# Changing the layout of y, the engine that stores results, and the order of the opening in a gated linear attention kernel with an MLP behind it

## The chip, the cores and the metric

One core of one Trainium2 chip. The metric is the device time of one execution in microseconds (us), as the median of three runs.

## The reference, cut to what matters

A recurrent attention over 768 tokens (4 batches, 8 heads, head size 48) with a decay per channel, and an MLP with a SiLU between two matrices (384 to 2048 to 384) on its 3072 output rows.

```python
B, H, S, D = 4, 8, 768, 48
f = 1.0 / (1.0 + np.exp(-f_logit))
for t in range(S):
    state = f[:, :, t, :, None] * state + np.einsum('bhd,bhe->bhde', k[:, :, t], v[:, :, t])
    y[:, :, t] = np.einsum('bhd,bhde->bhe', q[:, :, t], state)
x = y.transpose(0, 2, 1, 3).reshape(B * S, H * D)
h = x @ w_in
g = h * (1.0 / (1.0 + np.exp(-h)))
out = g @ w_out
```

## The kernel before, in words

The tokens are cut into 6 chunks (g) of 128 per batch; with 4 batches (b) there are 24 units (g, b). Heads are taken in pairs (p, 4 of them), two heads of 64 padded channels on the 128 partitions. For each unit:

- `decay` (L138): the log decays are summed over tokens by one matmul with a triangle (`cs`, one PSUM buffer); ACT makes exp(cs) and exp(-cs) from it (L144, L147); POOL scales k into `ki` (L145), DVE scales q into `qg` (L148). `values` (L150) casts v to bf16 on POOL, or on ACT where told.
- `transposes` (L171): 8 transposes into one PSUM buffer, evacuated by DVE (L178).
- `scores` (L181): 8 matmuls into one PSUM buffer; DVE masks them in two operations (`atm`, L190).
- `outputs` (L193): y is made with channels on partitions, ready to be the moving operand of the MLP, in 3 blocks of 128 channels. A head of 48 channels can straddle two blocks, so the v tile `vp` keeps zeros around every head and a window of 128 columns of it is the weight (10 matmuls), and the state tile `st` is 384 columns wide and zero outside the pair's block (6 matmuls, from chunk 1 on). DVE evacuates to `xT` (L209).
- `state` (L211): the old state goes into PSUM by a matmul with the identity (L217, from chunk 1 on), 4 matmuls add k times v (L220), and DVE multiplies by the chunk's last decay into `st` (L224, two operations).

The MLP: `mlp_in` (L252) does 3 matmuls for each of 16 blocks of hidden channels into one of two PSUM buffers (`h_ps`), ACT evacuates with SiLU (L266). `mlp_out` (L269) does 16 matmuls for each 128 rows into the same two buffers (`o_ps`), DVE copies to `o_sb` (three buffers, L278), and SP issues the store (L280). The loads of q, k, v and f are issued by SP too (L85), in program order with the stores, two buffers for each tensor; the weights are loaded by POOL (L109, L114).

The order on every engine is the order of the program. `run` interleaves streams: it always takes the next step of the stream that has used the smallest share of its stated cost. The costs (`T_COST` and so on, the numbers that the streams yield) have no other use. From chunk 1 on, while one chunk's `mlp_in` runs, half of the next chunk's attention (`attend`) is interleaved, and while its `mlp_out` runs, the other half together with `prep` (values, decay, lasts) of the chunk after that. `logs` (L129), which makes the log decays on ACT, needs the exp and ln tables, and stands ahead of that second half; SiLU needs other tables. Ahead of that loop an opening handles chunk 0 in two halves of two batches (FIRST, SECOND), then chunk 0's MLP and chunk 1.

Of the kernel before, what the change touches and what calls it, by code (L numbers as in the profile page):

```python
# [41 lines left out]
def kernel(  # L42
# [10 lines left out]
    nc = tc.nc  # L53
# [9 lines left out]
    VW = D + 128  # L63
# [34 lines left out]
    vp = [singles.tile([C, B, 128 + H * VW], BF16, name=f"vp{i}") for i in range(2)]  # L98
    st = [singles.tile([C, NP, HD], BF16, name=f"st{i}") for i in range(B)]
# [50 lines left out]
    def values(g, b, engine=None):  # L150
        src, dst = loaded[g, "v"][:, b], v_data(g % 2, b)
# [41 lines left out]
    def outputs(g, b):  # L193
        i = g % 2
        y_ps = yps.tile([128, KT, C], F32, name="y_ps", tag="yd")
        for t in range(KT):
            terms = []
            if g > 0:
                for p in range(NP):
                    if 2 * D * p < 128 * (t + 1) and 2 * D * (p + 1) > 128 * t:  # L200
                        terms.append((st[b][:, p, 128 * t:128 * (t + 1)], qkT[b][:, 0, p, :]))
            for h in range(H):
                if D * h < 128 * (t + 1) and D * (h + 1) > 128 * t:
                    terms.append((v_window(i, b, h, t), atm[b][:, h % 2, h // 2, :]))
            for n, (l, r) in enumerate(terms):
                nc.tensor.matmul(y_ps[:, t, :], l, r, start=(n == 0), stop=(n == len(terms) - 1))  # L206
        if g not in xT:
            xT[g] = gk.tile([128, KT, B, C], BF16, name="xT")
        nc.vector.tensor_copy(xT[g][:, :, b, :], y_ps)  # L209

    def state(g, b):  # L211
        i = g % 2
        flat = st[b].rearrange("p n w -> p (n w)")
        blocks = bass.AP(flat.tensor, flat.offset, [list(flat.ap[0]), [HD + 2 * D, NP], [1, 2 * D]])
        d_ps = yps.tile([128, NP, 2 * D], F32, name="d_ps", tag="yd")
        if g > 0:
            nc.tensor.matmul(d_ps, ident, blocks, start=True, stop=False, skip_group_check=True)  # L217
        vv = v_data(i, b)
        for p in range(NP):
            nc.tensor.matmul(d_ps[:, p, :], ki[i][:, b, 2 * p:2 * p + 2, :], vv[:, 2 * p:2 * p + 2],  # L220
                             start=(g == 0 and p == 0), stop=(p == NP - 1), skip_group_check=True)
        for r in range(2):
            lo = 64 * r
            nc.vector.tensor_mul(blocks[lo:lo + D, :, r * D:(r + 1) * D],  # L224
                                 d_ps[lo:lo + D, :, r * D:(r + 1) * D],
                                 alast[g][lo:lo + D, b, :, None].to_broadcast([D, NP, D]))

    T_COST, A_COST, Y_COST, D_COST = 450.0, 350.0, 900.0, 330.0

    def attend(g, lo, hi):  # L230

        units = range(lo, hi)
        for s in range(len(units) + 2):
# [35 lines left out]
    def mlp_out(g, lo, hi):  # L269
        for b in range(lo, hi):  # L270
            o_ps = hps.tile([C, d_model], F32, name="o_ps", tag="h_ps")
            for n in range(NT):
                nc.tensor.matmul(o_ps, hT[g][:, n, b * C:(b + 1) * C], w_out_sb[:, n, :],  # L273
                                 start=(n == 0), stop=(n == NT - 1))
                if n % 4 == 3 and n < NT - 1:
                    yield 650.0
            o_sb = op.tile([C, d_model], F32, name="o_sb")
            nc.vector.tensor_copy(o_sb, o_ps)  # L278
            r0 = b * S + g * C
            nc.sync.dma_start(out=out[r0:r0 + C, :], in_=o_sb)  # L280
            yield 650.0
# [4 lines left out]
    def prep(g, lo, hi):  # L286

        for b in range(lo, hi):
            values(g, b)
            decay(g, b)  # L290
            yield 200.0
        lasts(g, lo, hi)
        yield 120.0 * (hi - lo)

    def prep_cost(lo, hi):
        return (hi - lo) * 320.0
# [19 lines left out]
    def run(*streams):  # L316
        for _ in interleave_gen(*streams):
            pass

    with tc.manual_schedule():  # L320
# [15 lines left out]
        for b in range(*FIRST):  # L336
            values(0, b)
        logs(0, *SECOND)
        for b in range(*FIRST):
            transposes(0, b)  # L340
        for b in range(*SECOND):
            decay(0, b)
        for b in range(*FIRST):
            scores(0, b)
        load_w_in()
        for b in range(*FIRST):
            outputs(0, b)
# [11 lines left out]
        for b in range(*SECOND):  # L359
            outputs(0, b)  # L360
# [78 lines left out]
```

## Time and profile before

| what | us |
|---|---|
| median of 3 runs (lowest, highest) | 245.88 (244.97, 246.54) |
| the profiled execution | 248.17 |
| its span, from the first to the last instruction | 246.4 |

The rows below come from the profiled execution, whose time lies 1.8 us above its span. Engines: PE is the matrix engine (PEld its weight loads), DVE the vector engine, ACT the scalar engine, POOL GpSimd, SP the engine that only issues transfers (SPq, its queue). "PEclk" is the clock that was granted to PE, as a share of the full 2.4 GHz; 0.5 is the lower level, 1.2 GHz. A group row reads: line, engine, operation, output<-input, shapes, count | busy us, mean ns of one | idle time ahead of it <- what ended that.

### The profile page before, as it was taken

The numbers are of one execution on the slowest core, as the hardware profiler recorded it, in microseconds if no ns is written. First come the engines' busy times: TensorE is split into PE (matmuls) and PEld (weight loads), VectorE is DVE, ScalarE is ACT, GpSimd is POOL, SyncE is SP. The second block draws the span as 40 slices with busy tenths as digits, with TensorE's granted clock in tenths as the row PEclk, the third lists the DMA queues.
The fourth block names the chain that finished last, engine by engine and source line by source line (L and its number), as shares of the span: only waits on it lengthen the run. The fifth ranks groups of instructions, "written<-read, shape, count | busy, mean of one in ns | idle before, by whom it ended". The sixth has DMA issues, their size and how long they took to land.

```text
span 246.4 us, 4049 instructions
## 1 busy us (share of the span) xinstructions
PE 201.1 (82%) x1680; PEld 123.4 (50%) x1680; DVE 111.0 (45%) x193; ACT 114.3 (46%) x181; POOL 53.3 (22%) x65
## 2 busy tenths in 40 slices
PE   0346689968604896899779999999999999999994
PEld 0125534536304672687535565655666555663462
DVE  7727722246204544467655345763557453520011
ACT  4351237850410386348265683556735654008600
POOL 8629100050300006300190000900009100000000
PEclk9999769999965798589958999999999999999999
DMA  8999999999992000699409991179601100100011
GB/s 138 187 186 194 191 185 190 197 180 185 189 192 95 0 3 32 131 188 176 85 28 195 187 137 49 49 141 188 90 35 64 36 0 0 63 37 32 3 64 64
DMA packets 105971, 27.00 MB, mean 110 GB/s; under 512 B 99296, under 2 KB 105952, under 8 KB 105952
## 3 DMA queue, kind: packets, MB, share of 16 engines
q1 hardware_dynamic: 102272, 23.60, 60.3%
q0 software_dynamic: 3680, 3.15, 7.9%
q8 instruction: 13, 0.21, 0.4%
q14 instruction: 6, 0.05, 0.1%
HBM read 25.17 MB, written 4.72 MB: 121 GB/s over the span
## 4 chain that ended last, share of the span: by engine, by line
PE 77%; DMA 6%; DVE 5%; ACT 4%; SPq 4%; issue 2%; ACTq 0%; DVEq 0%
PE h_ps L263 29%; PE o_ps L273 25%; PE y_ps L206 9%; PE t_ps L176 5%; SPq L85 4%; PE a_ps L186 3%; DMA out_dram<-o_sb 3%; DMA q_ld<-in_q_dram 3%; DVE atm L190 2%; ACT ia L144 2%; PE cs L142 2%; ACT a L147 2%; PE d_ps L220 2%; DVE qk L178 1%; PE d_ps L217 1%
## 5 line engine op out<-in xcount | busy, mean ns | idle before, releaser
L266 ACT ACTIVATE hT<-h_ps 128x512 bf16<-128x512 f32 x96 | 57.3, 597 | 64.0 <-PE h_ps L263 62.0
L263 PE MATMUL h_ps<-xT,w_in_sb 128*128 128x512 bf16 (+1 forms) x336 | 79.6, 373 | 0.9 <-DVE xT L209 0.7
L273 PE MATMUL o_ps<-w_out_sb,hT 128*128 128x384 bf16 x384 | 72.0, 330 | 0.0
L273 PEld LDWEIGHTS <-hT 128*128 128x128 bf16 x384 | 35.9, 99 | 27.7 <-issue 7.2
L263 PEld LDWEIGHTS <-w_in_sb 128*128 128x128 bf16 x336 | 32.6, 104 | 29.5 <-issue 9.0
L145 POOL TENSOR_TENSOR ki<-k_ld,ia 128x384 bf16<-128x384 f32 x24 | 26.3, 1094 | 67.5 <-ACT ia L144 26.8
L190 DVE TENSOR_TENSOR atm<-a_ps,triu 128x512 bf16<-128x512 f32 x48 | 30.9, 685 | 17.6 <-PE a_ps L186 17.4
L278 DVE COPY o_sb<-o_ps 128x384 f32<-128x384 f32 x24 | 13.4, 556 | 44.9 <-PE o_ps L273 32.5
L155 POOL CAST vp<-v_ld 128x384 bf16<-128x384 f32 x22 | 15.1, 691 | 70.3 <-DMA v_ld<-in_v_dram 70.3
L144 ACT ACTIVATE ia<-cs 128x384 f32<-128x384 f32 x24 | 11.8, 490 | 33.2 <-PE cs L142 33.2
L148 DVE TENSOR_TENSOR qg<-q_ld,a 128x384 bf16<-128x384 f32 x24 | 17.9, 754 | 16.9 <-ACT a L147 12.0
L178 DVE COPY qk<-t_ps 128x1024 bf16<-128x1024 bf16 x24 | 16.6, 690 | 18.0 <-PE t_ps L176 18.0
L142 PE MATMUL cs<-lf,triu 128*128 128x384 bf16 x24 | 8.9, 369 | 18.5 <-ACT a L147 10.2
L206 PE MATMUL y_ps<-atm,vp 128*128 128x128 bf16 x240 | 23.7, 234 | 0.1
L224 DVE TENSOR_TENSOR st<-d_ps,al 48x192 bf16<-48x192 f32 x40 | 14.2, 354 | 21.0 <-PE d_ps L220 17.0
L176 PE MATMUL t_ps<-ident,qg 128*128 128x128 bf16 x96 | 11.3, 252 | 15.0 <-DVE qg L148 11.7
L176 PEld LDWEIGHTS <-qg 128*128 128x128 bf16 x96 | 8.8, 115 | 21.6 <-DVE qg L148 13.8
L209 DVE CAST xT<-y_ps 128x384 bf16<-128x384 f32 x24 | 13.3, 555 | 12.3 <-PE y_ps L206 12.3
L206 PEld LDWEIGHTS <-vp 128*128 128x128 bf16 x240 | 17.8, 106 | 0.5 <-issue 0.5
L206 PE MATMUL y_ps<-qk,st 128*128 128x128 bf16 x120 | 16.5, 219 | 0.0
L186 PE MATMUL a_ps<-qk 48*128 48x128 bf16 x192 | 10.2, 230 | 6.0 <-DVE atm L190 6.0
L186 PEld LDWEIGHTS <-qk 48*128 48x128 bf16 x192 | 5.8, 99 | 15.5 <-issue 7.7
(37 smaller groups left out, 126.6 us busy)
## 6 DMA issues: line engine op xcount, KB each, us to landing
out_dram<-o_sb SPq DMA_DIRECT2D x24, 192.0 KB, 1.9
f_ld<-in_f_logit_dram SPq DMA_DIRECT2D x4, 768.0 KB, 11.0
k_ld<-in_k_dram SPq DMA_DIRECT2D x4, 768.0 KB, 6.4
q_ld<-in_q_dram SPq DMA_DIRECT2D x4, 768.0 KB, 10.1
v_ld<-in_v_dram SPq DMA_DIRECT2D x4, 768.0 KB, 11.1
f_ld<-in_f_logit_dram SPq DMA_DIRECT2D x4, 384.0 KB, 6.7
k_ld<-in_k_dram SPq DMA_DIRECT2D x4, 384.0 KB, 6.7
q_ld<-in_q_dram SPq DMA_DIRECT2D x4, 384.0 KB, 6.8
```

Of the source, the lines that this page charges most:

```text
L144: nc.scalar.activation(ia, cs, AF.Exp, scale=1.0)
L145: nc.gpsimd.tensor_mul(ki[i][:, b, :, 0:D], loaded[g, "k"][:, b], ia)
L148: nc.vector.tensor_mul(qg[i][:, b, :, 0:D], loaded[g, "q"][:, b], a)
L155: nc.gpsimd.tensor_copy(dst, src)
L176: nc.tensor.transpose(t_ps[:, j, p, :], src[i][:, b, 2 * p:2 * p + 2, :], ident)
L178: nc.vector.tensor_copy(sb, t_ps)
L186: nc.tensor.matmul(a_ps[:, r, p, :], qkT[b][lo:lo + D, 1, p, :], qkT[b][lo:lo + D, 0, p, :], start=True, stop=True)
L190: nc.vector.tensor_mul(sb[:, r], a_ps[:, r], triu[:, None, :].to_broadcast([C, NP, C]))
L206: nc.tensor.matmul(y_ps[:, t, :], l, r, start=(n == 0), stop=(n == len(terms) - 1))
L263: nc.tensor.matmul(h_ps[:, j], w_in_sb[:, kk, (n + j) * 128:(n + j + 1) * 128], xT[g][:, kk, lo:hi].rearrange("p b c -> p (b c)"), start=( ...
L266: nc.scalar.activation(hT[g][:, n:n + per, lo * C:hi * C], h_ps, AF.Silu)
L273: nc.tensor.matmul(o_ps, hT[g][:, n, b * C:(b + 1) * C], w_out_sb[:, n, :], start=(n == 0), stop=(n == NT - 1))
```

## The change

y is made with tokens on partitions: 4 matmuls of 96 columns with the state, 8 of 48 columns with v; DVE (in the opening ACT) evacuates it to SBUF as bf16, three PE transposes turn it in a step of its own (`turn`), and another evacuation writes `xT`. `vp` becomes the dense `vb`, `st` the dense 96 columns for a pair. The old state is added by DVE to the PSUM result in place of the identity matmul. ACT copies `o_ps` out and issues the store. The opening does chunk 0 of FIRST through its scores before it starts SECOND's decay. All of chunk 2's loads and chunk 3's f are issued ahead of chunk 0's MLP. More of chunk 0's `mlp_out` (5850 in place of 3900) runs ahead of chunk 1's prep. The stated costs change: prep's steps are now spread over its stream.

```diff
-    vp = [singles.tile([C, B, 128 + H * VW], BF16, name=f"vp{i}") for i in range(2)]
-    st = [singles.tile([C, NP, HD], BF16, name=f"st{i}") for i in range(B)]
+    vb = [singles.tile([C, B, H, D], BF16, name=f"vb{i}") for i in range(2)]
+    st = [singles.tile([C, NP, 2 * D], BF16, name=f"st{i}") for i in range(B)]
...
-        y_ps = yps.tile([128, KT, C], F32, name="y_ps", tag="yd")
...
-                nc.tensor.matmul(y_ps[:, t, :], l, r, start=(n == 0), stop=(n == len(terms) - 1))
...
-        nc.vector.tensor_copy(xT[g][:, :, b, :], y_ps)
+        y_ps = yps.tile([C, H, D], F32, name="y_ps", tag="yd")
+        opened = False
+        for p in range(NP):
+            if g > 0:
+                nc.tensor.matmul(y_ps[:, 2 * p:2 * p + 2, :], qkT[b][:, 0, p, :], st[b][:, p, :],
+                                 start=not opened, stop=False, skip_group_check=True)
+                opened = True
+            for r in range(2):
+                nc.tensor.matmul(y_ps[:, 2 * p + r, :], atm[b][:, r, p, :], vb[i][:, b, 2 * p + r, :],
+                                 start=not opened, stop=True, skip_group_check=True)
+                opened = True
+        sb = wk.tile([C, HD], BF16, name="y")
+        evac(engine, sb, y_ps.rearrange("p h d -> p (h d)"))
+        ysb[b] = sb
+
+    def turn(g, b, engine=None):
+
+        x_ps = yps.tile([128, KT, C], BF16, name="x_ps", tag="yd")
+        for t in range(KT):
+            nc.tensor.transpose(x_ps[:, t, :], ysb[b][:, 128 * t:128 * (t + 1)], ident)
...
+        evac(engine, xT[g][:, :, b, :], x_ps)
...
-            nc.tensor.matmul(d_ps, ident, blocks, start=True, stop=False, skip_group_check=True)
...
+            src = wk.tile([128, NP, 2 * D], F32, name="sd")
+            nc.vector.tensor_add(src, d_ps, st[b])
...
-    T_COST, A_COST, Y_COST, D_COST = 450.0, 350.0, 900.0, 330.0
+    T_COST, A_COST, Y_COST, D_COST, X_COST = 450.0, 350.0, 400.0, 170.0, 170.0
...
-            if s >= 2:
+            if 2 <= s <= len(units) + 1:
                 outputs(g, units[s - 2])
...
+            if s >= 3:
+                turn(g, units[s - 3])
+                yield X_COST
...
-            nc.vector.tensor_copy(o_sb, o_ps)
+            nc.scalar.copy(o_sb, o_ps)
...
-            nc.sync.dma_start(out=out[r0:r0 + C, :], in_=o_sb)
+            nc.scalar.dma_start(out=out[r0:r0 + C, :], in_=o_sb)
...
-            yield 200.0
+            yield 1000.0
         lasts(g, lo, hi)
-        yield 120.0 * (hi - lo)
+        yield 100.0
...
-        nc.gpsimd.memset(vp[1], 0.0)
-        nc.vector.memset(vp[0], 0.0)
         for b in range(B):
-            nc.vector.memset(st[b], 0.0)
+            nc.gpsimd.memset(st[b], 0.0)
...
+        for b in range(*FIRST):
+            transposes(0, b)
         logs(0, *SECOND)
         for b in range(*FIRST):
+            scores(0, b)
+        for b in range(*SECOND):
+            decay(0, b)
+        load_w_in()
+        load_w_out()
+        for b in range(*FIRST):
+            outputs(0, b, nc.scalar)
+        for b in range(*SECOND):
             transposes(0, b)
...
-        load(2, "f")
-
-
-        run((mlp_in(0, *ALL), mlp_cost(*ALL)), (states(0, *ALL), B * D_COST))
-        for name in "kqv":
+        for name in "fkqv":
             load(2, name)
         load(3, "f")
+
+
+        run((mlp_in(0, *ALL), mlp_cost(*ALL)), (states(0, *ALL), B * D_COST))
...
-        run((part(out0, 3900.0), 3900.0))
+        run((part(out0, 5850.0), 5850.0))
...
-            (chain(wait(3000.0), prep(2, *ALL)), 3000.0 + prep_cost(*ALL)))
+            (chain(wait(1000.0), prep(2, *ALL)), 1000.0 + prep_cost(*ALL)))
...
-                lead = half if g == 1 else 1300.0
+                lead = half if g == 1 else 2000.0
```

## Rows read from the trace of the kernel before

**Rows 1.** The page: engines over the span, and the granted clock in 40 slices.
```profile
PE 201.1 (82%) x1680; PEld 123.4 (50%) x1680; DVE 111.0 (45%) x193; ACT 114.3 (46%) x181; POOL 53.3 (22%) x65
PEclk9999769999965798589958999999999999999999
```

**Rows 2.** Windows by stage: stretch, its length, busy us by engine, PEclk, DMA.
```profile
0.00:31.66 31.66, 12.36 (x125) 9.18 (x125) 19.84 (x29) 10.53 (x17) 18.41 (x25) 0.95 1.27 179
31.66:49.98 18.32, 18.25 (x93) 8.66 (x93) 3.40 (x9) 12.52 (x19) 0.50 (x1) 0.90 1.29 191
49.98:66.63 16.65, 11.81 (x130) 7.72 (x128) 8.26 (x14) 5.24 (x11) 5.42 (x7) 1.00 1.26 184
66.63:77.11 10.48, 0.84 (x14) 0.51 (x10) 1.89 (x5) 2.06 (x3) 1.02 (x2) 0.63 1.00 188
77.11:99.47 22.36, 19.32 (x169) 13.68 (x170) 10.35 (x18) 11.91 (x18) 5.21 (x6) 0.81 0.03 10
99.47:128.23 28.76, 24.92 (x249) 18.03 (x248) 16.75 (x30) 14.59 (x23) 7.95 (x10) 0.80 0.81 124
128.23:160.74 32.51, 32.06 (x281) 19.35 (x280) 17.68 (x33) 19.61 (x30) 7.66 (x9) 0.96 0.78 122
160.74:192.20 31.46, 30.88 (x281) 18.73 (x280) 17.63 (x33) 18.76 (x29) 7.13 (x8) 1.00 0.61 101
192.20:220.66 28.46, 28.35 (x242) 16.87 (x240) 12.40 (x21) 9.55 (x16) 0.00 (x0) 1.00 0.08 29
220.66:246.40 25.74, 22.34 (x112) 10.68 (x110) 2.79 (x5) 9.55 (x16) 0.00 (x0) 1.00 0.10 39
```

**Rows 3.** Windows inside these stages, same columns.
```profile
93.00:99.00 6.00, 3.59 (x19) 1.68 (x18) 2.94 (x6) 3.49 (x8) 4.74 (x5) 0.80 0.09 33
98.00:106.60 8.60, 7.82 (x64) 5.51 (x63) 4.03 (x6) 3.41 (x6) 2.89 (x4) 0.50 0.80 134
```

**Rows 4.** Timeline, 47 to 78 us: the first copy, the first stores, the stall's end.
```profile
48.07 0.56 DVE L278 COPY o_sb<-o_ps 128x384 f32<-128x384 f32 x1 [4.04 <-PE o_ps L273]
...
68.05 8.02 SPq L280 DMA_DIRECT2D out_dram<-o_sb  x4
...
75.15 0.56 DVE L278 COPY o_sb<-o_ps 128x384 f32<-128x384 f32 x1 [11.92 <-DMA out_dram<-o_sb]
...
77.11 0.61 PE L176 MATMUL t_ps<-ident,qg 128*128 128x128 bf16 x4 [9.64 <-DVE qg L148]
```

**Rows 5.** The stores' issue on SP: duration ns min/median/max, first and last start.
```profile
L280 SPq DMA_DIRECT2D out_dram<-o_sb x24: 332/333/4727, 68.0 to 243.6; - x24
```

**Rows 6.** Chain in order of time, full clock: start, us until the next piece, what.
```profile
108.98 0.89 PE y_ps L206 x16
...
110.52 0.16 PE d_ps L217
...
111.51 0.45 PE t_ps L176 x8
```

**Rows 7.** Timeline, 66 to 67 us: eight loads of weights with one-column matmuls.
```profile
66.45 0.34 PE L161 MATMUL al_ps<-ones,lf 128*128 128x1 bf16 x8 [1.02 <-ACT a L147]
```

**Rows 8.** Groups by line and shape.
```profile
L161 PE MATMUL al_ps<-ones,lf 128*128 128x1 bf16 x96 | 3.6, 165 | 1.4 <-ACT a L147 1.4
...
L209 DVE CAST xT<-y_ps 128x384 bf16<-128x384 f32 x24 | 13.3, 555 | 12.3 <-PE y_ps L206 12.3
...
L144 ACT ACTIVATE ia<-cs 128x384 f32<-128x384 f32 x24 | 11.8, 490 | 33.2 <-PE cs L142 33.2
L178 DVE COPY qk<-t_ps 128x1024 bf16<-128x1024 bf16 x24 | 16.6, 690 | 18.0 <-PE t_ps L176 18.0
L148 DVE TENSOR_TENSOR qg<-q_ld,a 128x384 bf16<-128x384 f32 x24 | 17.9, 754 | 16.9 <-ACT a L147 12.0 <-DMA q_ld<-in_q_dram 3.4 <-ACT ia L144 1.0
L124 ACT ACT_TABLE_LOAD x6 | 7.7, 1283 | 0.8 <-PEq L423 0.7
L135 ACT ACTIVATE e<-f_ld 128x1536 f32<-128x1536 f32 x4 | 5.9, 1483 | 0.0
```

More of the change, by code (lines that the diff above doesn't have):

```diff
@@ L62 @@
     MT = B * C
-    VW = D + 128
     singles = ctx.enter_context(tc.tile_pool(name="singles", bufs=1))
@@ L150, in values @@
     def values(g, b, engine=None):
-        src, dst = loaded[g, "v"][:, b], v_data(g % 2, b)
+        src, dst = loaded[g, "v"][:, b], vb[g % 2][:, b]
         if engine is nc.scalar:
@@ L191, in scores @@
         atm[b] = sb
-    def outputs(g, b):
-        i = g % 2
-        y_ps = yps.tile([128, KT, C], F32, name="y_ps", tag="yd")
-        for t in range(KT):
[L197 to L205, printed above, removed]
-                nc.tensor.matmul(y_ps[:, t, :], l, r, start=(n == 0), stop=(n == len(terms) - 1))
+    ysb = {}
@@ new lines, in evac, with outputs @@
+    def evac(engine, dst, src):
+        if engine is nc.scalar:
+            nc.scalar.copy(dst, src)
+        else:
+            nc.vector.tensor_copy(dst, src)
+    def outputs(g, b, engine=None):
+        i = g % 2
+        y_ps = yps.tile([C, H, D], F32, name="y_ps", tag="yd")
[12 more added lines that the diff above has]
+        ysb[b] = sb
@@ L214, in state @@
-        blocks = bass.AP(flat.tensor, flat.offset, [list(flat.ap[0]), [HD + 2 * D, NP], [1, 2 * D]])
         d_ps = yps.tile([128, NP, 2 * D], F32, name="d_ps", tag="yd")
+        for p in range(NP):
+            nc.tensor.matmul(d_ps[:, p, :], ki[i][:, b, 2 * p:2 * p + 2, :], vb[i][:, b, 2 * p:2 * p + 2],
+                             start=True, stop=True)
+        src = d_ps
         if g > 0:
-            nc.tensor.matmul(d_ps, ident, blocks, start=True, stop=False, skip_group_check=True)
@@ L218, in state @@
[L218 to L221, printed above, removed]
+            src = wk.tile([128, NP, 2 * D], F32, name="sd")
+            nc.vector.tensor_add(src, d_ps, st[b])
         for r in range(2):
             lo = 64 * r
-            nc.vector.tensor_mul(blocks[lo:lo + D, :, r * D:(r + 1) * D],
-                                 d_ps[lo:lo + D, :, r * D:(r + 1) * D],
+            nc.vector.tensor_mul(st[b][lo:lo + D, :, r * D:(r + 1) * D],
+                                 src[lo:lo + D, :, r * D:(r + 1) * D],
@@ L226, in state @@
                                  alast[g][lo:lo + D, b, :, None].to_broadcast([D, NP, D]))
-    T_COST, A_COST, Y_COST, D_COST = 450.0, 350.0, 900.0, 330.0
+    T_COST, A_COST, Y_COST, D_COST, X_COST = 450.0, 350.0, 400.0, 170.0, 170.0
     def attend(g, lo, hi):
         units = range(lo, hi)
-        for s in range(len(units) + 2):
+        for s in range(len(units) + 3):
             if s < len(units):
@@ L290, in prep @@
             decay(g, b)
-            yield 200.0
+            yield 1000.0
         lasts(g, lo, hi)
-        yield 120.0 * (hi - lo)
+        yield 100.0
     def prep_cost(lo, hi):
-        return (hi - lo) * 320.0
+        return (hi - lo) * 1000.0 + 100.0
     def wait(cost):
@@ L337 @@
             values(0, b)
+        for b in range(*FIRST):
+            transposes(0, b)
         logs(0, *SECOND)
         for b in range(*FIRST):
-            transposes(0, b)
+            scores(0, b)
         for b in range(*SECOND):
             decay(0, b)
+        load_w_in()
+        load_w_out()
         for b in range(*FIRST):
[L344 to L347, printed above, removed]
+            outputs(0, b, nc.scalar)
         for b in range(*SECOND):
             transposes(0, b)
+        for b in range(*FIRST):
+            turn(0, b, nc.scalar)
         for b in range(*SECOND):
             values(0, b, nc.scalar)
-        load_w_out()
         for span in (FIRST, SECOND):
@@ L359 @@
         for b in range(*SECOND):
-            outputs(0, b)
+            outputs(0, b, nc.scalar)
+        for b in range(*SECOND):
+            turn(0, b, nc.scalar)
         for t in (lf[1], qg[1], ki[1], lf[2]):
             nc.gpsimd.memset(t[:, :, :, D:64], 0.0)
-        load(2, "f")
-        run((mlp_in(0, *ALL), mlp_cost(*ALL)), (states(0, *ALL), B * D_COST))
-        for name in "kqv":
+        for name in "fkqv":
             load(2, name)
         load(3, "f")
+        run((mlp_in(0, *ALL), mlp_cost(*ALL)), (states(0, *ALL), B * D_COST))
         exp_ln_tables()
@@ L372 @@
         out0 = mlp_out(0, *ALL)
-        run((part(out0, 3900.0), 3900.0))
+        run((part(out0, 5850.0), 5850.0))
         run((part(out0, 1950.0), 1950.0), (prep(1, *FIRST), prep_cost(*FIRST)))
-        run((out0, mlp_cost(*ALL) - 5850.0), (attend(1, *FIRST), attend_cost(1, *FIRST)))
+        run((out0, mlp_cost(*ALL) - 7800.0), (attend(1, *FIRST), attend_cost(1, *FIRST)))
         logs(1, *SECOND)
```

8 lines of the change are left out of this document (1 added, 7 removed).

## The prediction, made before the changed kernel was built or run

> **What bounds the kernel now.** I read the page first. PE is busy for 201.1 of 246.4 us, the other engines for less than half of the span, so the sum of PE's work is the first suspect; but the granted clock dips several times [rows 1]. The windows by stage then show where PE is not the bound. Three kinds of stretch stand out [rows 2]. Up to 66.6 us PE is busy 42 of 67 us, beside transfers at 180 to 190 GB/s: data and short dependent chains. From 66.63 to 77.11 it works for 0.84 us: a stall. From 77 to 128 it is busy 44 of 51 us, but at a mean clock of 0.8. Behind 128 us it is busy 95 to 100% at almost full clock; there the time is PE's work.
>
> The timeline explains the stall [rows 4]. The first result was copied at 48.07, its store was issued at 68.05, because SP works in order and all of chunk 2's loads stood ahead of it. There are three `o_sb` buffers, so the fourth copy sat on DVE until the first store had landed, and behind it on DVE the scaled q, for which PE's transposes waited until 77.11. The dips have a second cause beside that stall: the four decays of `prep` come at the end of their stream, one behind the other through the single `cs` buffer; in such a burst PE is busy for 3.59 of 6 us, and then runs at 1.2 GHz for 8.6 us [rows 3].
>
> **The change part by part.**
>
> PE, for one unit. Sixteen matmuls take 0.89 us from start to next start, the identity matmul 0.16, eight transposes 0.45 [rows 6]. The new y has 4 matmuls of 96 columns, 8 of 48 columns and 3 transposes. Three transposes are 3/8 of 0.45, 0.17. 128 columns go in 0.89/16 = 0.056, so 96 in about 0.042, four in 0.17. For 48 columns the weight load may set the pace: eight one-column matmuls with as many loads take 0.34 us with the last one's 0.165, so (0.34 - 0.165)/7 = 0.025 a pair [rows 7, 8]; the upper bound is the 0.056 of a 128-column pair. Eight cost 0.20 to 0.45; I take 0.20, as the row with the least columns shows what a load allows and 48 columns alone are 0.021. So y falls from 0.89 to 0.54, with the upper bound to 0.79. With the identity matmul a unit saves 0.35 + 0.16 = 0.51 (0.26 at the bound), without state (chunk 5) 0.35.
>
> The Trainium skill (TensorE: Matmul & The Clock Gate, LDWEIGHTS (loading the stationary operand)) gives a load as its columns over 1.2 GHz, an estimate of 107 ns for 128. By it fifteen loads would take 1.6 us a unit, y would be dearer by 0.7, and 20 units would add 14 us in place of saving 7, and the time would be some 242. The trace does not agree: sixteen loads and matmuls went by in 0.89 us [rows 6].
>
> DVE, for one unit. The `xT` evacuation of 0.555 is replaced by the same for y, and a second one from bf16. That lies between 0.555 and the 0.690 of the 1024-column bf16 copy scaled to 384 columns, 0.26; I take 0.36, nearer the bf16 row. The addition of the state is a 384-column tensor operation, 0.754 in the mean where POOL disturbs it; 0.56 without [rows 8]; I take 0.56. DVE gains 0.92 and loses one `o_sb` copy of 0.56 [rows 4]: net 0.36 a unit. Hidden behind 128 us, where it is busy 17.6 of 31.5 [rows 2]. Between 99 and 128 it has four units and only two copies to lose: 16.75 + 4 x 0.92 - 2 x 0.56 = 19.3 us, and that stage can't get shorter than this.
>
> ACT, for each 128 rows: a 384-column copy from PSUM, 0.49 as `ia` [rows 8], and the issue, 0.33 to 4.73 [rows 5]. I take 0.33, the median. Four times 0.82 in a chunk is 3.3 beside 18.8 busy of 31.5 [rows 2]: hidden. Queued behind an issue on ACT are the exps of the next decay, for which PE's next `cs` waits. Loads pass SP without waiting for results now; they can only come earlier.
>
> The opening. SECOND's decay moves behind FIRST's scores, so SECOND's `cs` waits for DVE's mask: about 1 us later on PE, ACT, POOL, and the weights' transfers, issued behind POOL's `ki`, shift with it. But FIRST's y no longer waits for SECOND's q, and `vp`'s memsets are gone. I expect the first `h_ps` at 29 in place of 31.66, between 28 and 32. Little of it survives: `mlp_out` now does 8 more matmuls ahead of prep, and chunk 1's first half is a chain through one `t_ps` buffer, one `a_ps` buffer and DVE, with 2.6 us of MLP left to cover it; PE is the bound there in 11.81 of 16.65 us only [rows 2]. I take 0.3 us gained at 66.6 (between -3 and 3).
>
> 66.6 to 99.5. The stall goes: 10.48 - 0.84 = 9.6. The dip behind it and the burst's: the mean clock of 0.81 over 19.3 busy us is worth 3.7; I take back 2.7. The burst's idle time, 2.4 [rows 3]. Two units, 1.0. What is late next: `prep` now starts after 1000 of its stated 5100, some 2 us into the stage, but its first `cs` needs ACT's table load and the two log passes, 1.28 + 1.48 + 1.48 us [rows 8] behind the last SiLU. PE meets that wait with the MLP and the attention queued behind it: +3.3. Sum -12.4.
>
> 99.5 to 128.2. Clock: 0.2 x 24.9 = 5.0, of which I take 4.0. PE's idle time is 28.76 - 24.92 = 3.8, of which I take 3.1 for the second burst of decays. Four units, 2.0. Against it 1.0 for the logs (prep starts at 43% now) and 1.0 for DVE, which is close to its 19.3 us. Sum -7.1, to 21.7 us.
>
> 128.2 to 160.7: clock 1.0 of the 1.3 that 0.96 costs, four units 2.0, 0.2 back for the logs: -2.8. To 192.2: four units 2.0, 0.4 back: -1.6. To 220.7: 4 x 0.35, and 0.4 back, as `turn` is now the last thing ahead of the next `mlp_in`: -1.0. The rest, 25.74, stays: the final copy moves between engines at 0.56 against 0.49, and SP's issue becomes ACT's.
>
> Sum: -0.3 - 12.4 - 7.1 - 2.8 - 1.6 - 1.0 = -25.2. The span goes from 246.4 to 221.2, the profiled execution (1.8 around the span) from 248.2 to 223.0. The median of the runs stands 0.9% under the profiled execution, so 221.
>
> **The rivals.**
>
> The clock stays low. Each part of the attention has less PE work beside it, and new waits (the logs, DVE) can make PE idle where it is busy now; the dips in the trace came behind stretches of 60% busy [rows 3]. For it: the 3.3 us wait. Against it: bursts and stall, behind which all late dips began, are gone. Then the 2.7, 4.0 and 1.0 are not taken back: 221 + 7.7 = 229.
>
> Stores still wait for loads, now in ACT. SP's loads run on while ACT issues, and one store behind a load took 4.73 us to issue [rows 5]. If ACT's issue waits similarly behind the others' backlog, the four stores between 77 and 128 us, where ACT paces the decays, cost half of 4.4 each: +9, 230. Against it: 4.73 was seen on the loads' own queue, and the median is 0.33. The Trainium skill (DMA: Bandwidth & Descriptors, Issuing engines are not separate DMA queues) says that another issuing engine saves only the issue time, usually small. By it the stall's 9.6 would mostly stay, again about 230; the trace shows a store ready at 48.6 and issued at 68.05, so here that time was large [rows 4].
>
> The other side: the same wait in full. If each of the eight stores issued while loads queue holds ACT for 4.4 us more, none of it covered, that is 35 us, 256. It turns slower than before from 25/8 = 3.1 us a store. Nothing in the trace shows a foreign queue doing that.
>
> The weights set the pace. With 0.056 for every 48-column pair, a unit saves 0.26 in place of 0.51: 20 units, 5 us, 226.
>
> The change does not do what it says: the stall is replaced by another of its size, because chunk 2's data are what PE really waits for at 67 us. Then prep of chunk 2 would wait; but transfers end by 77 us in the trace, and that prep is at 76 at the earliest. 232.
>
> **How the numbers follow.** The forecast 0.60; low clock 0.14; stores half 0.10; weights 0.06; chunk 2's data 0.03; no gain, 244 to 248, by several of them together 0.02; stores in full 0.05. Below 221 lie a stage 77 to 128 without DVE's and the logs' waits (-5.3) and the whole clock (-2.3) and opening (-2.7), 211 at the best. The range, 211 to 233, leaves out the stores in full, the no-gain case and the tails, about 0.15. A measurement of this kernel tells about 1% from no change: faster 0.93, within 1% 0.02, slower 0.05.
>
> **What would show it.** Right: no idle PE stretch of 10 us near 67; the DVE wait for a store gone; y as 12 matmuls in 0.54 us; the last `mlp_in` starting near 195 and 25.7 us from there to the end; a PE wait of about 3 us for the logs of chunk 2. The opening is right if `h_ps` starts near 29 and chunk 1's second half near 66. The clock: right if under 10 us at the lower level remain behind 66 us. Wrong: issues on ACT of over 1 us while SP loads; DVE busy all through a chunk's attention; a new wait for a load.

## The result, and the profile after

| | before | after |
|---|---|---|
| median of 4 runs on one chip (lowest, highest), us | 245.81 (244.97, 246.54) | 231.16 (230.86, 232.45) |
| ratio to before, 95% interval | | 0.941 [0.935, 0.947] |
| profiled execution, its span, us | 248.17, 246.4 | 232.45, 230.7 |

The kernel is 14.7 us faster; I had forecast 24.9. Some executions of a kernel run 1 to 3% longer at a lower granted clock; the times and ratios below leave them out. A profile is that of one execution; the one of after is the longest of its four, 1.3 us over the median, and two executions of one kernel can differ by a microsecond at a stage's border. The page of after, against [rows 1]: PE is busy for 10.5 us less, ACT for 13.9 more, and one slice at the lower level of the clock (5) is left of three.

```profile
PE 190.6 (83%) x1648; PEld 113.5 (49%) x1648; DVE 112.3 (49%) x196; ACT 128.2 (56%) x213; POOL 49.6 (22%) x68
...
PEclk9999999999958978899979999999999999999999
```

The windows by stage of after, with the columns of [rows 2] (stretch, length, busy us of PE, PEld, DVE, ACT, POOL, then PEclk, DMA share, GB/s). A stage begins with the first `h_ps` of chunk 0, of chunk 1's first two batches, of its other two, and of chunks 2, 3, 4 and 5. The MLP of chunk 1's first half runs beside the attention of its second half, so the stage from 65.88 is the one that I call "chunk 1's second half" in the forecast.

```profile
0.00:27.68 27.68, 11.84 (x128) 8.18 (x129) 12.14 (x20) 12.61 (x25) 14.96 (x28) 1.00 1.29 179
27.68:65.88 38.20, 30.58 (x218) 16.09 (x218) 13.82 (x28) 20.82 (x35) 6.16 (x8) 0.97 1.27 204
65.88:90.96 25.08, 19.22 (x176) 13.46 (x174) 13.12 (x21) 15.72 (x25) 8.41 (x10) 0.84 1.34 195
90.96:117.16 26.20, 21.53 (x240) 15.46 (x240) 20.20 (x36) 13.90 (x22) 6.01 (x8) 0.89 0.83 134
117.16:147.60 30.44, 29.39 (x279) 17.14 (x276) 20.98 (x37) 20.61 (x35) 7.83 (x10) 0.98 0.62 104
147.60:177.36 29.76, 28.81 (x272) 17.01 (x272) 20.45 (x36) 20.34 (x33) 6.24 (x8) 1.00 0.08 28
177.36:204.60 27.24, 26.92 (x236) 15.38 (x236) 11.58 (x20) 12.34 (x21) 0.00 (x0) 1.00 0.08 30
204.60:230.70 26.10, 22.28 (x114) 10.78 (x112) 0.00 (x0) 11.83 (x21) 0.00 (x0) 1.00 0.10 38
```

Against the forecast's own stages:

| stage | before | forecast | after |
|---|---|---|---|
| start to first `h_ps` | 31.7 | 29 | 27.7 |
| chunk 1's second half starts at | 66.7 | 66.3 | 65.9 |
| that stage (65.88 to 90.96 in after) | 32.8 | 20.4 | 25.1 |
| the next stage, to chunk 2's first `h_ps` | 28.8 | 21.7 | 26.2 |
| the next three | 32.5, 31.5, 28.5 | 29.7, 29.9, 27.5 | 30.4, 29.8, 27.2 |
| the rest | 25.7 | 25.7 | 26.1 |

So everything is within 1.4 us of its forecast but two neighbouring stages, 65.88 to 117.16. They took 51.3 us where I had 42.1: 9.2 us of the miss lie there. In four stretches of them PE, busy all the time, runs at the lower level of the clock:

```profile
65.88:70.40 4.52, 4.52 (x32) 3.46 (x30) 1.77 (x2) 2.65 (x4) 0.66 (x1) 0.50 1.35 200
80.80:84.20 3.40, 3.40 (x26) 2.18 (x24) 2.45 (x5) 1.07 (x3) 1.78 (x2) 0.50 1.43 187
91.00:94.40 3.40, 3.40 (x22) 2.70 (x22) 0.69 (x1) 1.24 (x2) 0.00 (x1) 0.51 1.13 214
115.00:117.16 2.16, 2.16 (x24) 1.29 (x23) 1.71 (x5) 1.10 (x3) 0.88 (x1) 0.50 0.00 0
```

That is 13.5 us at half speed, 6.7 us lost. A stage's mean clock (0.84, 0.89) counts PE's idle time too and shows less of it. So what the clock costs is taken below from windows of half a microsecond, as PE's busy time times what the clock lacks of 1: 4.1 us in the first of the two stages, 2.8 in the second.

Two rows of after bear out the prices for PE and for the logs. The timeline shows a unit's y as 12 matmuls (4 with the state, each followed by 2 with v) between two of the MLP, and PE waiting for chunk 2's logs:

```profile
75.84 0.21 PE L201 MATMUL y_ps<-st,qk 128*128 128x96 bf16 x1
...
76.16 0.21 PE L205 MATMUL y_ps<-vb,atm 128*128 128x48 bf16 x2
76.21 0.81 PE L285 MATMUL o_ps<-w_out_sb,hT 128*128 128x384 bf16 x4
80.34 0.32 PE L135 MATMUL cs<-lf,triu 128*128 128x384 bf16 x1 [3.32 <-ACT lf L129]
```

From the first of the twelve to the MLP's next start are 0.37 us; I had 0.17 + 0.20 = 0.37. The wait is 3.32; I had 3.3 for the first stage.

The chain that ended last, 106 to 117 us, shows what I did not have. Each piece is start, us until the next, what:

```profile
106.53 0.49 ACT o_sb L290
107.04 0.34 ACTq L292
...
107.48 0.49 ACT ia L137
107.97 0.39 ACT a L140
108.39 1.08 DVE qg L141
109.46 0.48 DVE sd L230
109.97 1.04 DVE st L233
111.02 0.57 DVE st L233
...
111.61 0.36 DVE xT L192
112.00 1.40 DVE qg L141
113.41 0.47 DVE y L192
113.87 0.47 DVE qg L141
114.34 0.48 DVE sd L230
```

From 106.53 to 114.8 PE is not in the chain at all. Two of its waits there:

```profile
109.98 0.20 PE L201 MATMUL y_ps<-st,qk 128*128 128x96 bf16 x1 [1.25 <-DVE sd L230]
...
113.93 0.33 PE L216 MATMUL x_ps<-ident,y 128*128 128x128 bf16 x3 [0.92 <-DVE y L192]
```

A result is copied and stored on ACT, the decay's exps wait behind it, DVE scales q when they are done, and the addition, the state and `xT`, for which PE waits, stand behind that q on DVE. Every link is one that the change made or moved.

### The profile page after: what moved, and what is told of

Read it like the earlier page. It is cut to its first block, busy times and chain, and to the rows that moved or that the text cites. A ratio compares the mean times of both kernels' runs of the same rounds, so it can differ in the third digit from the quotient of the medians.

```text
span 230.7 us, 4001 instructions
## 1 busy us (share of the span) xinstructions
PE 190.6 (83%) x1648; PEld 113.5 (49%) x1648; DVE 112.3 (49%) x196; ACT 128.2 (56%) x213; POOL 49.6 (22%) x68
## 4 chain that ended last, share of the span: by engine, by line
PE 52%; ACT 15%; DVE 12%; DMA 12%; issue 3%; POOL 2%; ACTq 1%; SPq 1%; DVEq 0%
PE h_ps L275 23%; PE o_ps L285 17%; DMA w_out_sb<-in_moe_w_out_dram 9%; DVE qg L141 4%; PE t_ps L169 4%; DMA q_ld<-in_q_dram 3%; PE a_ps L179 3%; DVE st L233 2%; ACT e L128 2%; ACT o_sb L290 2%; ACT ia L137 2%; DVE atm L183 2%; ACT hT L278 2%; ACT a L140 2%; ACT L278 2%
## 5 line engine op out<-in xcount | busy, mean ns | idle before, releaser
L285 PE MATMUL o_ps<-w_out_sb,hT 128*128 128x384 bf16 x384 | 73.9, 331 | 0.2
L278 ACT ACTIVATE hT<-h_ps 128x512 bf16<-128x512 f32 x96 | 56.9, 597 | 27.9 <-PE h_ps L275 26.2
L275 PEld LDWEIGHTS <-w_in_sb 128*128 128x128 bf16 x336 | 32.5, 103 | 33.1 <-issue 12.2
L285 PEld LDWEIGHTS <-hT 128*128 128x128 bf16 x384 | 35.2, 99 | 26.5 <-issue 7.1
L141 DVE TENSOR_TENSOR qg<-q_ld,a 128x384 bf16<-128x384 f32 x24 | 22.9, 959 | 29.1 <-ACT a L140 20.4
L290 ACT COPY o_sb<-o_ps 128x384 f32<-128x384 f32 x24 | 11.4, 477 | 34.7 <-PE o_ps L285 34.7
L148 POOL CAST vb<-v_ld 128x384 bf16<-128x384 f32 x22 | 15.8, 721 | 24.9 <-DMA v_ld<-in_v_dram 24.9
L233 DVE TENSOR_TENSOR st<-sd,al 48x192 bf16<-48x192 f32 x32 | 14.0, 438 | 1.0
L169 PEld LDWEIGHTS <-qg 128*128 128x128 bf16 x96 | 8.3, 110 | 10.2 <-DVE qg L141 4.5
L128 ACT ACTIVATE e<-f_ld 128x768 f32<-128x768 f32 (+1 forms) x8 | 9.3, 1163 | 7.0 <-DMA f_ld<-in_f_logit_dram 6.6
L205 PEld LDWEIGHTS <-atm 128*128 128x128 bf16 x192 | 10.3, 101 | 5.5 <-issue 3.7
L192 DVE CAST y<-y_ps 128x384 bf16<-128x384 f32 x20 | 11.0, 551 | 3.6 <-PE y_ps L205 3.5
L205 PE MATMUL y_ps<-vb,atm 128*128 128x48 bf16 x192 | 12.0, 191 | 0.4 <-DVE atm L183 0.4
L140 ACT ACTIVATE a<-cs 128x384 f32<-128x384 f32 x24 | 11.6, 485 | 0.0
```

Source lines behind the costliest of these rows:

```text
L141: nc.vector.tensor_mul(qg[i][:, b, :, 0:D], loaded[g, "q"][:, b], a)
L169: nc.tensor.transpose(t_ps[:, j, p, :], src[i][:, b, 2 * p:2 * p + 2, :], ident)
L205: nc.tensor.matmul(y_ps[:, 2 * p + r, :], atm[b][:, r, p, :], vb[i][:, b, 2 * p + r, :], start=not opened, stop=True, skip_group_check=True)
L233: nc.vector.tensor_mul(st[b][lo:lo + D, :, r * D:(r + 1) * D], src[lo:lo + D, :, r * D:(r + 1) * D], alast[g][lo:lo + D, b, :, None].to_br ...
L275: nc.tensor.matmul(h_ps[:, j], w_in_sb[:, kk, (n + j) * 128:(n + j + 1) * 128], xT[g][:, kk, lo:hi].rearrange("p b c -> p (b c)"), start=( ...
L278: nc.scalar.activation(hT[g][:, n:n + per, lo * C:hi * C], h_ps, AF.Silu)
```

## The experiments

All times are medians; each ratio is to the kernel before, run beside it on the same chip. "The two stages" are those from 65.88 to 117.16 in after, from the first `h_ps` of chunk 1 to that of chunk 2: 61.4 us before (66.66 to 128.03), 51.3 after. The store edit, the order of prep and the addition of the state were undone or tried alone; the layout of y, the opening and the earlier loads were not.

**Which edit removed the stall?** First the store edit alone, on the kernel before:

```diff
-            nc.vector.tensor_copy(o_sb, o_ps)
+            nc.scalar.copy(o_sb, o_ps)
-            nc.sync.dma_start(out=out[r0:r0 + C, :], in_=o_sb)
+            nc.scalar.dma_start(out=out[r0:r0 + C, :], in_=o_sb)
```

> The kernel before with one edit: ACT copies the result and issues the store; layout, opening and prep as before. Undoing that edit in the changed kernel cost 14 us (245.0 against 231). If the edit carries nearly the whole gain and the rest nets nothing, this kernel takes 231 to 234. If the parts need each other (the stall only becomes worth 14 us because the rest runs earlier), it takes 235 to 240, the 9.6 us of PE idle time being all that goes; the new y would then show as the difference.

238.5 us, ratio 0.975 [0.963, 0.987], the second of the two cases. In its profiled execution (238.0) the two stages fall from 61.4 to 46.9: the stall is gone. But the stage ahead of them grows by 2.9, to 37.9, and the later three are 31.9, 32.1 and 29.7 for 32.5, 31.5 and 28.5. So 14.5 are gained in place and some 4 paid back around it. And 46.9 is less than after's 51.3: in the two stages the rest of the change loses 4.4, if single executions may be compared so.

Then everything but the store edit (`nc.vector.tensor_copy` and `nc.sync.dma_start` put back in the kernel after):

> Undone alone: DVE copies the result and SP issues the store, behind chunk 2's loads. If ACT's stores are what removed the stall, DVE waits for the first store near 60 to 75 us again: 9 to 12 us more, 240 to 243. If the stall would have gone anyway (chunk 0's MLP runs earlier now), the time stays at 229 to 233.

244.98 us, 1.003 [0.998, 1.008]: no change that can be measured, and 2 us above the range that I gave for it. The timeline, SP, DVE and PE:

```profile
63.84 4.11 SPq L84 DMA_DIRECT2D f_ld<-in_f_logit_dram  x1
68.04 8.20 SPq L292 DMA_DIRECT2D out_dram<-o_sb  x4
...
75.32 0.56 DVE L290 COPY o_sb<-o_ps 128x384 f32<-128x384 f32 x1 [13.39 <-DMA out_dram<-o_sb]
...
76.53 0.48 PE L216 MATMUL x_ps<-ident,y 128*128 128x128 bf16 x3 [14.21 <-DVE sd L230]
```

The stores are issued at 68.04, where [rows 4] have 68.05. The stall's end is set here by the queue of loads and not by compute, so all that the new layout and opening gain ahead of it turns into waiting: 13.39 us of it in place of 11.92. The store edit alone gives 2.5%, the rest alone nothing, both together 5.9%: the rest is worth something here only where nothing downstream waits for a transfer. The Trainium skill (DMA: Bandwidth & Descriptors, Issuing engines are not separate DMA queues) has another issuing engine save only the time that the issue takes, usually small beside the transfer. That agrees here in its letter, as what the stores escape is SP's queue; that this is small does not: it is the 14 us between this kernel and after.

Last the copy alone put back on DVE, the issue left on ACT:

> DVE copies the result again, ACT still issues the store. If ACT's order holds the decays (a copy of 0.48 waiting for PE ahead of the next exp, six times between 76 and 117 us), the time falls by 1 to 3 us, to 228 to 230. If DVE's order does, 0.56 for each of 4 copies there are added to the chain: 233 to 235. No difference would say that neither queue's length matters.

236.99 us, 0.974 [0.968, 0.980]. It loses about 6 us to after, more than either case had. The stage from 27.68 grows by 1.1, the later three to 31.9, 31.1 and 28.1 from 30.4, 29.8 and 27.2; the two stages stay at 50.9. So the copy on ACT pays in the full stages, where DVE is busy some 20 of 30 us and its order still costs 1.4 in two of the three periods, and pays nothing in the two stages, where half an MLP is all that PE has besides the attention (they are called thin below) and ACT is in the chain as well.

**Where did the two stages lose 9 us?** Prep's stated costs and leads as before, for all chunks:

```diff
-            yield 1000.0
+            yield 200.0
         lasts(g, lo, hi)
-        yield 100.0
+        yield 120.0 * (hi - lo)
...
-            (chain(wait(1000.0), prep(2, *ALL)), 1000.0 + prep_cost(*ALL)))
+            (chain(wait(3000.0), prep(2, *ALL)), 3000.0 + prep_cost(*ALL)))
...
-                lead = half if g == 1 else 2000.0
+                lead = half if g == 1 else 1300.0
```

> Undone alone: prep's stated costs and leads (200 a batch and 120 a batch behind them, leads of 3000, half and 1300), so that the decays come late and close together again. Between 66 and 117 us the changed kernel took 51.1 us where I had forecast 42. If the early start of prep is what costs there (PE waits 3.32 us for chunk 2's logs, and each scaled q stands ahead of the attention's evacuations on DVE), the time falls by 3 to 6 us, to 225 to 228. If the burst costs more than that wait, as forecast (PE idle 2 to 3 us in each chunk's second half and a lower clock behind it in two of them), it rises by 4 to 8, to 235 to 239.

231.0 us, 0.949 [0.942, 0.956]: neither theory's number, the same time as after by another way (the two intervals overlap; its profile is of the shortest of its executions, after's of the longest, so some 2 us of what the windows differ by are not in the medians). Its windows of the two stages and the next:

```profile
66.84:87.34 20.50, 16.96 (x177) 12.21 (x173) 11.61 (x21) 15.22 (x25) 7.32 (x8) 0.92 1.27 186
87.34:111.86 24.52, 20.49 (x241) 14.94 (x240) 19.49 (x36) 14.43 (x22) 7.39 (x10) 0.92 1.17 179
111.86:144.62 32.76, 31.27 (x271) 18.20 (x272) 21.26 (x37) 20.64 (x34) 8.63 (x10) 0.92 0.59 97
```

The two stages take 45.0, 6.3 less than after: 4.6 in the first, 1.7 in the second. In the first stage, chunk 2's first decay now comes behind the logs, and PE's wait for them is down to one for an exp:

```profile
82.05 0.32 PE L135 MATMUL cs<-lf,triu 128*128 128x384 bf16 x1 [1.22 <-ACT a L140]
```

PE's idle time there falls from 5.9 to 3.5, and what the clock costs from 4.1 to 1.4. But the stage behind the two gives 2.3 back. Its windows of 4 us show why:

```profile
108.00:112.00 4.00, 1.86 (x25) 1.20 (x24) 3.96 (x7) 2.22 (x5) 4.00 (x5) 0.81 0.63 84
112.00:116.00 4.00, 3.78 (x15) 1.88 (x15) 1.50 (x2) 2.60 (x4) 1.17 (x2) 0.50 0.88 181
```

In the burst of decays PE is busy 1.86 of 4 us, DVE and POOL all the time, and behind it PE runs at the lower level. Over that stage the clock costs 2.6, where it costs after 0.6. Chunk 1 begins 1.0 later, and the period of chunk 3 is 0.7 longer. So the spread of prep, which I had booked as a gain throughout, loses in the two thin stages and gains behind them.

The identity matmul in place of DVE's addition, for all chunks:

```diff
+            nc.tensor.matmul(d_ps, ident, st[b], start=True, stop=False, skip_group_check=True)
...
-            src = wk.tile([128, NP, 2 * D], F32, name="sd")
-            nc.vector.tensor_add(src, d_ps, st[b])
```

> Undone alone: the old state goes into PSUM by an identity matmul again (st stays dense), DVE's addition is gone. If DVE's order is what holds PE between 76 and 117 us, each of the 6 units there loses 0.55 us of addition, and st from PSUM takes 0.35 in place of 0.44 to 0.8: 3 to 5 us less there, against 0.16 us of PE for each of 12 units behind it, 2: the time is 228 to 230. If DVE has slack, 16 identity matmuls of 0.16 are on the path: 233 to 234.

231.92 us, 0.951 [0.944, 0.958]. Level with after again, between the two cases, and again of two signs: the two stages take 48.0 (-3.3, of it -2.6 in the second), the next periods 31.0, 30.3 and 27.6 (+0.6, +0.5, +0.3), and chunk 1's second half begins 1.8 later, of which over 1 us can be chance (the same kernel began it at 67.0 and 65.9 in two executions, below). An identity matmul takes the 0.16 that was forecast, 0.64 a chunk; the +0.5 is at full clock in both, the +0.6 is not, and chunk 5's period has none. The six additions of 0.55 that go from the two stages are 3.3 as well, but that they agree is chance: PE's idle time falls by 0.9 there, its work grows by 1.1, and the clock costs 3.5 less (3.3 in place of 6.9, table in the next section).

Now both put back only in the two thin stages (the identity also for the two units just ahead of them), late prep for chunks 2 and 3 (first kernel), and also the identity matmul for chunks 1 and 2 (second):

```diff
+        late = g in (2, 3)
...
-            yield 1000.0
+            yield 200.0 if late else 1000.0
...
+        early = g <= 2
+        if early and g > 0:
+            nc.tensor.matmul(d_ps, ident, st[b], start=True, stop=False, skip_group_check=True)
...
-        if g > 0:
+        if not early:
```

> The changed kernel with prep of chunks 2 and 3 alone late and close together, as before; chunks 1, 4 and 5 keep the spread. With all preps undone the stretch from chunk 1's first MLP to chunk 2's took 45.0 us in place of 51.3, and the next two periods 63.2 in place of 60.2. If these two add up, spreading is bad where half an MLP is beside it and good where a whole one is: 225 to 228. If the long periods were only longer because they began earlier (a wait for loads), it stays at 230 to 232.

> As the one with prep of chunks 2 and 3 late, and the states of chunks 1 and 2 take the old state by an identity matmul again, chunks 3 and 4 by DVE. With the identity everywhere, 66 to 117 us was 3.3 us shorter beside a spread prep. If DVE's length is a bound there by itself, it gives 2 to 3 us more than late prep alone, 223 to 225. If the late prep already took that wait away, it gives 0 to 1.

228.86 us, 0.936 [0.929, 0.943], and 225.95 us, 0.924 [0.914, 0.934], each about a microsecond above its range. The second is the best kernel of this study, faster than after and than the first mix. Of the 2.9 us that it gains on that mix, the two stages have only 1.3 (44.3 in place of 45.6) and the stage behind them 2.0: what the clock cost there, 2.8, is gone. Run once more on another chip it took 225.21, 0.919 [0.912, 0.925]; the windows of the two stages and the next one, of that run:

```profile
65.88:87.95 22.07, 19.40 (x179) 13.79 (x176) 10.44 (x19) 14.85 (x23) 7.33 (x8) 0.81 1.27 196
87.95:110.32 22.37, 20.10 (x244) 14.49 (x244) 16.81 (x32) 14.73 (x23) 6.22 (x8) 0.98 1.12 182
110.32:140.43 30.11, 28.65 (x276) 17.02 (x275) 20.95 (x37) 20.38 (x34) 9.18 (x12) 1.00 0.65 106
```

44.4 us for the two stages, and the second of them at 22.4, close to the 21.7 that I had forecast; in the first execution they took 21.1 and 23.2. The next stage runs at full clock in both, although prep is late as in the kernel with the dip at 112 us; why this one keeps its clock was not tested.

**An attempt that gave nothing.** On top of the first mix, the logs of chunk 1's second half ahead of the rest of chunk 0's `mlp_out`, its prep beside chunk 1's first attention, and chunk 2's logs ahead of chunk 1's `mlp_in`, so that no logs stand in the middle of a stage:

```diff
         run((part(out0, 5850.0), 5850.0))
+        logs(1, *SECOND)
...
-        run((out0, mlp_cost(*ALL) - 7800.0), (attend(1, *FIRST), attend_cost(1, *FIRST)))
-        logs(1, *SECOND)
-        run((prep(1, *SECOND), prep_cost(*SECOND)))
+        run((out0, mlp_cost(*ALL) - 7800.0), (attend(1, *FIRST), attend_cost(1, *FIRST)),
+            (chain(wait(800.0), prep(1, *SECOND)), 800.0 + prep_cost(*SECOND)))
+        logs(2, *ALL)
```

> As the one with prep of chunks 2 and 3 late, and the logs of chunk 1's second half and of chunk 2 run on ACT while it idles beside chunk 1's first attention; prep of chunk 1's second half is interleaved there too. If the wait of PE for these logs and decays is on the path (near 50 to 66 and 76 to 80 us), it saves 3 to 6 us on top: 220 to 224. If loads are what chunk 2 then waits for (its f is issued at 49 and lands near 60), nothing, 225 to 228.

230.35 us, 0.942 [0.935, 0.950], beside 228.86 for the mix on the same chip: above both cases, a loss, if any change. Chunk 1's second half begins at 67.7 in place of 66.6, where PE waits for `xT`; 3.0 us of log passes stand ahead of its first SiLU, for which PE waits another 0.75; the two stages take 46.1 for 45.6. In the mix PE had no wait for the logs of chunk 2 left that this run could take away.

**A suspicion that gave nothing in the sum.** At each chunk's end ACT's last copy and issue stand ahead of the load of SiLU's table. In the best kernel, the last 128 rows of chunks 2 to 4 on DVE and SP again:

```diff
+            if 2 <= g < NCH - 1 and b == B - 1:
+                nc.vector.tensor_copy(o_sb, o_ps)
+                nc.sync.dma_start(out=out[r0:r0 + C, :], in_=o_sb)
```

> The same kernel as e6_mix_ident (late prep for chunks 2 and 3, identity matmul for chunks 1 and 2), as the yardstick for e8_last_row: 226 us, 225 to 227.

> e6_mix_ident, but the last 128 rows of chunks 2, 3 and 4 are copied by DVE and stored by SP, as in the kernel before; SP's loads are all issued by then. Theory: ACT's copy and issue of a chunk's last rows (0.49 + 0.34 us) stand ahead of the load of SiLU's table and of the first hT of the next chunk, and PE, with both h_ps buffers full, waits for them; three boundaries times 0.5 to 1.0 us, so 1.5 to 3 us less, 223 to 224.5. Rival: the wait at a boundary comes from the table load and the first SiLU alone, or DVE, busy with the last y and turn there, copies later than ACT would: within 0.5 us of e6_again, or up to 1 us slower.

225.01 us against 225.21: no difference that can be measured, as the rival had it. The two timelines, first the yardstick's and then that with the last rows on DVE:

```profile
169.31 0.48 ACT L294 COPY o_sb<-o_ps 128x384 f32<-128x384 f32 x1 [0.53 <-PE o_ps L289]
169.82 0.34 ACTq L296 DMA_DIRECT2D out_dram<-o_sb  x1
...
170.40 1.28 ACT L282 ACT_TABLE_LOAD   x1
```

```profile
170.17 1.28 ACT L282 ACT_TABLE_LOAD   x1
...
170.36 0.54 DVE L296 COPY o_sb<-o_ps 128x384 f32<-128x384 f32 x1
```

The table load stands 0.20 us behind the chunk's first `h_ps` (170.20) in the yardstick and 0.32 ahead of it (170.49) in the other, so a half microsecond was gained on ACT; PE was waiting 0.56 us for DVE's `xT` at that place in both, and the wait for the first SiLU behind it was 0.24 us in the yardstick. That wait did go: from chunk 2 to chunk 5 PE waits 1.3 us for SiLUs in the yardstick and not at all in the other, and the periods of chunks 3 and 4 are 0.4 us shorter each (29.4 and 26.9). But the lower clock costs PE 1.0 us more in chunk 2's period, ahead of the first of the edited rows, and the granted clock of a whole execution is 0.967 to 0.976 in all four where the yardstick has 0.977 to 0.985. Why, stays open.

## Why the prediction was right or wrong

The time lies inside the range of 211 to 233, near its end, which the rivals had set; the sum behind 221 was 9.5 us short.

**The stall.** Right. No idle stretch of 10 us is left, and DVE waits for no store. The run without the store edit has it back at 14.21 us of PE's time, the run of the store edit alone has none.

**PE's work.** Right for y (0.37 with 0.17 + 0.20 forecast; the sign that I gave, 12 matmuls in 0.54, counts the three transposes in) and for the identity matmul (0.16). The later three stages came out at -2.1, -1.7 and -1.2 for -2.8, -1.6 and -1.0. Weights at 0.056 a pair, the rival of 226, are refuted by the twelve matmuls in 0.37 us. The Trainium skill (TensorE: Matmul & The Clock Gate, LDWEIGHTS (loading the stationary operand)) gives a load as its columns over 1.2 GHz, an estimate of 107 ns for 128. The trace agrees for one load, 95 to 152 ns with a median of 96 for those of L205; that loads add up one behind the other, as I had it there, does not follow from it: twelve would take 1.3 us, and they went by in 0.37.

**The store on ACT.** The issue never waited: 0.338 to 0.373 us for all 24, with SP's loads beside it. Both store rivals (230, 256) fall. But "hidden" was wrong in the thin stages: copy and issue, 0.49 + 0.34, stand in the chain ahead of the exps at 107.48 (and at 84.92, further up in it). I had named the exps as what queues behind an issue, and put no price on it.

**The opening.** 27.7 for 29, a little below the 28 that I gave as its edge, and 65.9 for 66.3. Of 4.0 us gained at the first `h_ps` 0.8 survived, as argued.

**66 to 117 us.** This is the step that failed: in the sums -12.4 and -7.1, the term of 1.0 for DVE and the 2.7 and 4.0 taken back from the clock. The forecast left PE idle for 12.7 - 9.6 - 2.4 + 3.3 = 4.0 in the first stage and 3.8 - 3.1 + 1.0 + 1.0 = 2.7 in the second. The table sets the two stages together beside the runs: PE's waits by what ended them (logs, an exp, DVE), what the clock costs by windows of half a microsecond, and what is left, PE's work at full clock. Waits under 0.2 us are left out.

| us | the two stages | logs | exps | DVE | clock | PE's work |
|---|---|---|---|---|---|---|
| forecast | 42.1 | 4.3 | 1.4, not told apart | 1.0 | 2.0 | 33.4 |
| after | 51.3 | 3.3 | 1.5 | 5.8 | 6.9 | 33.9 |
| prep late, all chunks | 45.0 | 0 | 6.0 | 1.3 | 3.0 | 34.4 |
| prep late, chunks 2 and 3 | 45.6 | 0 | 6.0 | 1.3 | 3.5 | 34.4 |
| identity, all chunks | 48.0 | 3.6 | 1.7 | 4.2 | 3.3 | 34.9 |
| best kernel, first execution | 44.3 | 0 | 4.5 | 0.9 | 3.6 | 35.2 |
| best kernel, again | 44.4 | 0 | 4.3 | 0.4 | 4.6 | 34.9 |

So of the 9.2 us the waits for DVE have 4.8 and the clock 4.9; the logs give 1.0 back, PE's work adds 0.5. The terms for the stall and the logs of the first stage were right, and so were DVE's prices for y, `xT` and the sum (0.55, 0.36, 0.55). What I left out: the spread decays do not only remove a burst, each of them puts a chain through ACT and DVE into the middle of a stage in which half an MLP is all that PE has besides. I priced DVE by its sum (19.3 us as the second stage's floor; it came to 20.2), while its order decides: a scaled q that waits for an exp stands ahead of the sum, the state and `xT` of the unit at work. Late prep takes 4.5 of PE's waits for DVE away and the wait for the logs, and pays for it with 4.5 more behind exps, in its burst; the identity matmul alone takes 1.6 of the waits for DVE, both together some 5. With both, 7 of the 9.2 us are gone. How much of the waits for DVE is the order and how much the longer operations beside POOL (last section) no run separates.

I had the clock come back because "bursts and stall, behind which all late dips began, are gone". Some 15 us at the lower level remain behind 66 us, where I had named under 10 as the sign of being right, and each stretch of them begins behind thin work: in the 4 us ahead of 63.6, 80.8, 91.0 and 114.8 us PE was busy for 1.7, 0.7, 2.4 and 1.8. That suggests that the waits were paid for twice, once as idle time and once behind it, but how much of the clock comes back with them is not shown: the best kernel is idle for half of after's time there, and the clock still costs it 3.6 and 4.6 in two executions, the larger part of it up to 71 or 72 us, behind the decays of chunk 1's second half. The attempt that set those decays beside the attention kept this stretch, and what would take it away stays open.

**The rivals.** "The clock stays low", 229, described part of it: new waits for logs and DVE make PE idle where each part of the attention has less PE work beside it. Of its 7.7 us 5.2 came (7.5 lost over the three stages where the forecast left 2.3). It lacked the idle time itself. Chunk 2's data delayed nothing: the only wait for a load in the two stages is POOL's for v, of 4.3 us, and PE waited for no load.

**From span to time.** The span was 9.5 us over my 221.2, the median 10.2 over 221: the median lay 0.6% under the profiled execution, not 0.9%.

## What to carry to other kernels

Price an engine's new work by who waits behind it in its queue, not by the engine's busy share: here DVE was busy 20 of 26 us, its new work was priced at 1.0 us, and PE waited 5.8 us for it in two stages. An order that spreads work evenly suits the stages in which the big engine covers it, and is best chosen stage by stage: the same two edits lost in the thin stages about what they gained elsewhere. And the wait that ended with a transfer swallowed every gain ahead of it here, so remove that wait first, or measure the other edits with it gone.

## What the runs showed of the hardware

**A queue's backlog belongs to the engine that issues.** All 24 stores issued by ACT took 0.34 to 0.37 us to issue (the row gives ns min/median/max). Five of them, at 46.23, 48.20, 51.84, 60.67 and 84.48 us, began while SP was held in issuing a load, which took it 2.1 to 4.4 us; the last of the five:

```profile
L292 ACTq DMA_DIRECT2D out_dram<-o_sb x24: 338/338/373, 46.2 to 227.9; - x24
...
DMA to landing us min/median/max: 1.9/1.9/5.9
```

```profile
81.08 4.07 SPq L84 DMA_DIRECT2D f_ld<-in_f_logit_dram  x1
...
84.48 0.34 ACTq L292 DMA_DIRECT2D out_dram<-o_sb  x1
```

The landing took 3.3 to 5.9 us for the stores ahead of 66 us and 1.9 to 2.7 behind 125, after SP's last load: the transfers do meet the loads, the issue does not. I had given half of that wait a chance of 0.10.

**DVE slows beside POOL when all its sources are in SBUF, and not when one is in PSUM.** The DVE rows of after by line (ns min/median/max) show it:

```profile
L141 DVE TENSOR_TENSOR qg<-q_ld,a x24: 544/1074/1404, 9.0 to 176.0; 128x384 bf16<-128x384 f32 x24
...
L230 DVE TENSOR_TENSOR sd<-d_ps,st x16: 542/548/558, 58.8 to 174.2; 128x384 f32<-128x384 f32 x16
...
L233 DVE TENSOR_TENSOR st<-sd,al x32: 349/355/1068, 59.5 to 175.1; 48x192 bf16<-48x192 f32 x32
...
L233 DVE TENSOR_TENSOR st<-d_ps,al x8: 349/355/361, 29.6 to 40.5; 48x192 bf16<-48x192 f32 x8
```

`qg` and `sd` both work on 128x384; `qg`, from two tensors in SBUF, takes 0.54 to 1.40 us, `sd`, with one in PSUM, always 0.55. The state's product goes up to 1.07 from SBUF and to 0.36 from PSUM. After's own products from PSUM all lie where POOL rests, but in the run with the identity everywhere they lie where those from SBUF lie here, and stay short:

```profile
L232 DVE TENSOR_TENSOR st<-d_ps,al x40: 335/356/361, 30.2 to 174.3; 48x192 bf16<-48x192 f32 x40
```

The slow ones lie where POOL works: the `qg` of 1.08 at 108.39 has POOL's scaled k (108.05, 1.00) and v (108.99, 0.84) beside it. The `sd` that the chain has at 109.46 runs beside the same v, at its usual length. In these rows the one that begins second waits: every `qg` of chunks 1 to 5 that took over 0.6 us began with a POOL operation under way that ran on for 0.3 us or more beside it; those at 51.47 and 87.17 began at the end of one and just ahead of the next, and took 0.56, while that next one took POOL 1.35 us in place of 0.99. The median of `qg` was 0.56 before and is 1.07 now, in the late-prep kernel 1.02. So the addition had a second price that I had not seen: it moves the state's source from PSUM to SBUF. The Trainium skill (SBUF — State Buffer, 🔬 SBUF: two separate sides) has it that DVE operations with two SBUF inputs and GpSimd's reads share a pair of ports that one of them holds for a whole instruction; these rows agree, with up to 0.85 us lost by one operation. No run took POOL's work away.
